# Threshold attention and a squared-ReLU MLP on one core: values taken one step later, and their loads moved behind the last placing

## The chip, the cores and the metric

The kernel runs on one core of a Trainium2 chip. The metric is the device time of one execution in microseconds. The kernel before takes 1539.25 us (median of three runs, 1538.57 to 1540.27); its profiled execution has a span of 1535.8 us.

## The reference

Two stages, all in 32-bit floats. The first is attention with a threshold: 8 batches of 8 heads, 576 rows of 64 elements each. A score counts only if it is within tau (0.02) of the largest of its row.

```python
scores = scale * np.matmul(q, k.transpose(0, 1, 3, 2))
thresh = np.max(scores, axis=-1, keepdims=True) - tau
scores = np.where(scores >= thresh, scores, -1000000000.0)
scores = scores - np.max(scores, axis=-1, keepdims=True)
attn = np.exp(scores)
attn = attn / (np.sum(attn, axis=-1, keepdims=True) + 1e-09)
attn_out = np.matmul(attn, v)
```

The second takes the heads of a token side by side as a row x of 512 elements (4608 tokens) and computes `np.maximum(x @ w_in, 0) ** 2 @ w_out`, with w_in 512 x 2048 and w_out 2048 x 512.

## The kernel before

**Visits and steps.** Two heads make a pair, and there are 32 pairs, four to a batch. A *visit* works on one pair; the first eight visits share out the first batch's four pairs, so there are 36 visits (n from 0). A whole visit has five *steps* (i from 0 to 4). Steps 0 to 3 take 128 queries of each head of the pair; step 4 takes the 64 queries that are left of both heads together, by way of the tile `qmid`, and so has half the work. Further down, "step 4" is always a visit's last.

**One step.** `scores` (L201) multiplies queries with all 576 keys into PSUM tiles s0 and s1, which exist once, and DVE takes each row's maximum (L206). `exponents` (ACT, L214 to L217) writes the exponentials to a tile w. `threshold` (DVE, L229 to L232) compares, masks and sums; after it s0 and s1 are free again. `divide` (GpSimd, L239 to L241) normalizes w.

**Turning the weights.** The product with the values needs w transposed, with keys on the partitions, in the tile `wT`, which exists once. In early visits PE does this. From visit 11 on (`by_dma(n)`: 25 visits) DVE turns blocks of 32 x 32 one step later (`turn_blocks`, L296) into the tile `turned`, and DMAs put them where they belong (`place_blocks`): when step 3 has been turned, which is in step 4, sixteen transfers place all the blocks of steps 0 to 3 at once (L307, 144 KB each), and when step 4 has been turned, which is in step 0 of the next visit, sixteen smaller ones place what is left (L314, 16 or 20 KB each). The blocks of step 4 are turned into the tile `ql`, which the queries came in and which is free by then.

**Taking the values.** `mix` (L357) multiplies `wT` with the values of the pair, `vs[n % 2]`, in 20 matmuls over two PSUM banks, and `put` copies the result to the ring `xT` (ACT, L333 to L344), from which the MLP reads. The lists `mixes` says in which step it is done: `mixed = {NBLK: (0, 4)}` means all columns at once, four steps after the visit's step 4, so in step 3 of the next visit. In the step's text it stands right behind `scores` and `exponents`.

**Loads.** All of these transfers are issued by the queue of the SP engine, one after another in the order of the program. Queries and keys of the next visit (`load_qk`, L162 and L164, ten transfers) are asked for in step 2 and transposed by DVE in step 4 (`prep`, L180), after `threshold` and ahead of that step's `turn_blocks`. Values (`load_v`, L172 and L175, six transfers) are asked for at the end of step 4, for the next visit; in the queue they stand behind L307 and ahead of L314.

**The MLP as a filling.** The tokens are cut into 18 chunks of 256. When the mix of a batch's last pair is done, its chunks are complete (`complete`, `chunk_at`) and their *pieces* are added to a waiting list: `mlp_in` (L399) and `product` (L466, seven products in place of eight on halves of the matrices), each of eight matmuls in the profile's count. `fill` emits pieces between the parts of a step, a quarter of the step's share each time. The share comes from `rate`: the work at hand, spread over the steps up to the next chunk, less `VALUES_US` (4.8) in a step that has a mix. `END` is the step of the last mix; what still waits then is emitted behind it.

The order of each engine's instructions is the order of this text (a manual schedule). A step's text, cut to the change:

```python
scores(s) ... exponents(n, i)
if s in mixes and not old:
    mix(*mixes[s])              # then add_chunk(...)
fill(quarter)
threshold(n, i); prep(n + 1)    # prep in step 4
turn_blocks(m, x)               # of the step before
if x >= NBLK - 1:
    place_blocks(m, x)
fill(quarter) ... divide(n, i) ... fill(quarter); fill(quarter)
elif last and more and n >= 2 * HP:
    load_v(n + 1)
```

Of the kernel before, what the change touches and what calls it, by code (L numbers as in the profile page):

```python
# [19 lines left out]
def kernel(  # L20
# [15 lines left out]
    HP = H // 2  # L36
    NPAIR = B * HP
    NBLK = S // P
# [39 lines left out]
    at = RAW * 2 * WP  # L78
# [45 lines left out]
    def round_weights(i, stage):  # L124

        words = weight_area(i).bitcast(U32).rearrange("p (n w) -> p n w", w=2)
        lo, hi = words[:, :, 0], words[:, :, 1]  # L130
        t, e, d = (turned[:, (i % 3 * 3 + x) * WP:(i % 3 * 3 + x + 1) * WP] for x in range(3))
        tu, eu = t.bitcast(U32), e.bitcast(U32)
        if stage == 0:
            nc.scalar.activation(out=e, in_=hi.bitcast(FP32), func=AF.Copy, scale=2.0 ** -112)
            nc.scalar.activation(out=d, in_=lo, func=AF.Copy, scale=2.0 ** -52)
        elif stage == 1:
            nc.vector.tensor_scalar(out=tu, in0=hi, scalar1=0x80000000, scalar2=None, op0=ALU.bitwise_and)
            nc.vector.scalar_tensor_tensor(out=tu, in0=eu, scalar=3, in1=tu, op0=ALU.logical_shift_left,  # L138
                                           op1=ALU.bitwise_or)
        elif stage == 2:  # L140
            nc.vector.tensor_scalar(out=eu, in0=tu, scalar1=0xFF800000, scalar2=None, op0=ALU.bitwise_and)  # L141
        elif stage == 3:
            nc.gpsimd.tensor_tensor(out=d, in0=d, in1=e, op=ALU.mult)  # L143
        else:
            nc.gpsimd.tensor_tensor(out=weight_piece(i)[1], in0=t.rearrange("p (h d) -> p h d", h=2),
                                    in1=d.rearrange("p (h d) -> p h d", h=2), op=ALU.add)
# [4 lines left out]
    def load_qk(n):  # L151


        b, h = divmod(visits[n][0], HP)
        h *= 2
        for x, t in list(zip(rows_of(n), (q, k)))[::-1]:
            for m in range(4):
                queue = nc.scalar if n == 0 and m % 2 else nc.sync
                src = t[b, h + m // 2, :, (m % 2) * 32:(m % 2) * 32 + 32].rearrange("(c p) d -> p c d", p=32)
                last = REST // 32 if t is k and m >= 2 else 0  # L160
                to = x[m * 32:(m + 1) * 32, :, :]
                queue.dma_start(out=to[:, last:, :], in_=src[:, 0:S // 32 - last, :])  # L162
                if last:
                    queue.dma_start(out=to[:, 0:last, :], in_=src[:, S // 32 - last:, :])  # L164
# [12 lines left out]
    def prep(n):  # L177

        for to, rows in zip((qT, kT), rows_of(n)):
            nc.vector.transpose(to, rows.rearrange("p c d -> p (c d)"))  # L180
        if NBLK in visits[n][1]:
            for u in range(2):
                rows = slice(u * D, (u + 1) * D)
                nc.gpsimd.tensor_copy(out=qmid[rows, u * D:(u + 1) * D], in_=qT[rows, NBLK * P:S])  # L184
# [3 lines left out]
    def scores(s):  # L188

        vis, i = steps[s]  # L190
        n = 2 if i < NBLK else 1
        sc = [psum.tile([P, 2, 512], FP32, tag=f"s{u}", name=f"s{u}") for u in range(n)]
        halves = [(half, u) for half in range(2) for u in range(n)]
        if early():
            halves.sort(key=lambda x: x[1])
        for half, u in halves:
            if i < NBLK:
                rows, lhsT = slice(u * D, (u + 1) * D), qT[u * D:(u + 1) * D, i * P:(i + 1) * P]
            else:
                rows, lhsT = slice(0, P), qmid  # L200
            nc.tensor.matmul(sc[u][:, half, 0:HALF], lhsT, kT[rows, half * HALF:(half + 1) * HALF],  # L201
                             start=True, stop=True)
        st = pool.tile([P, 7, 2], FP32, tag="st", name="st", bufs=4)
        mx = st[:, 0, 0:n]
        for u in range(n):
            nc.vector.tensor_reduce(out=mx[:, u:u + 1], in_=sc[u][:, :, 0:HALF], axis=AX.XY, op=ALU.max)  # L206

        w = w_slots[(s - first_dma) % (2 if by_dma(vis) else 3)][:, 0:n, :]
        weights[vis, i] = w, sc, st

    def exponents(vis, i):
        w, sc, st = weights[vis, i]
        mx, thr, bias = (st[:, j, 0:len(sc)] for j in range(3))
        nc.scalar.activation(out=bias, in_=mx, func=AF.Copy, scale=-SCALE)  # L214
        nc.scalar.activation(out=thr, in_=mx, func=AF.Identity, bias=ntau8)
        for u in range(len(sc)):
            nc.scalar.activation(out=w[:, u, :].rearrange("p (h k) -> p h k", h=2), in_=sc[u][:, :, 0:HALF],  # L217
                                 func=AF.Exp, bias=bias[:, u:u + 1], scale=SCALE)
# [288 lines left out]
    def by_dma(n):  # L507

        return n >= 3 * HP - 1
# [6 lines left out]
    for s, (n, i) in enumerate(steps):  # L516

        if by_dma(n):
            mixed = {NBLK: (0, 4)}
        else:  # L520
            mixed = {x: (x, 3) for x in range(NBLK + 1)}
        if i in mixed:
            first, lag = mixed[i]
            cols = slice(first * P, min((i + 1) * P, S))
            mixes[s + lag] = (n, cols)
            g_ = visits[n][0]
            if g_ % HP == HP - 1:
                complete[s + lag] = g_ // HP * S + cols.stop
# [12 lines left out]
    def early():  # L541
        return state["step"] < min(chunk_at)
# [10 lines left out]
    def add_chunk(j):  # L553
        waiting.extend(pieces_of(j))
# [65 lines left out]
    for s in range(END + 1):  # L620
        state["step"] = s
        state["usable"] = rounded_by[-1]
        rounded_by.append(state["rounded"])
        on = s < NST
        now = []
        if on:
            n, i = steps[s]
            at = visits[n][1].index(i)
            last = at == len(visits[n][1]) - 1
            now = list(range(done, done + pieces[s]))  # L630
            done += pieces[s]
            more = n + 1 < len(visits)
            short = n < 2 * HP
            if short and at == 0 and 0 < n + 1 < 2 * HP:
                load_qk(n + 2)
            elif not short and at == (2 if by_dma(n) else 1) and more:
                load_qk(n + 1)
            if now:
                round_weights(now[0], 0)
            scores(s)  # L640
        old = steps[s - 2] if 2 <= s < NST + 2 and not by_dma(steps[s - 2][0]) else None
        at_once = now or old or early()
        lay = on and last and more and not by_dma(n)
        if old:
            turn(*old, 0)
            turn(*old, 1)
        if on:
            exponents(n, i)
            if lay:
                prep(n + 1)  # L650
            elif now:
                round_weights(now[0], 1)
        if s in mixes and not old:
            mix(*mixes[s])
            for j in chunk_at.get(s, ()):
                add_chunk(j)
        quarter = rate(s) / 4 if s < END else 1e9
        fill(quarter)
        if s in mixes and old:
            mix(*mixes[s])  # L660
            for j in chunk_at.get(s, ()):
                add_chunk(j)
        if old:
            turn(*old, 2)
        state["free"] = s > first_dma
        if on:
            threshold(n, i)
            if last and more and not lay:
                prep(n + 1)
            if lay and now:  # L670
                round_weights(now[0], 1)
            if now:
                round_weights(now[0], 2)
                round_weights(now[0], 3)
            if not at_once:
                divide(n, i)
        if 0 < s <= NST and by_dma(steps[s - 1][0]):
            m, x = steps[s - 1]
            turn_blocks(m, x)
# [3 lines that stand above are left out]
        if on and at_once:  # L683
            divide(n, i)
        fill(quarter)
        fill(quarter)
        if on:
            if now:
                end_rounding(now[0])
            for p in now[1:]:  # L690
                for stage in range(4):
                    round_weights(p, stage)
                end_rounding(p)
            if at == 0 and 0 < n <= 2 * HP:
                load_v(n)
            elif last and more and n >= 2 * HP:
                load_v(n + 1)
    after()
    after()
# [33 lines left out]
```

## Time and profile before

| engine | busy us | share of the span |
|---|---|---|
| PE, matmuls | 1416.3 | 92% |
| PEld, weight loads | 1086.5 | 71% |
| DVE | 864.7 | 56% |
| GpSimd | 670.5 | 44% |
| ACT | 439.7 | 29% |

Weight loads run beside matmuls. Other rows of the page: L201 has 178.3 us of matmuls, L399 520.1 us, and L466 250.4 and 187.9 us in two groups. In the chain of work that ended last PE holds 42% of the span and the SP queue 31%: L307 17%, L314 14%.

Three stretches can be told apart. Up to about 280 us weights are loaded and rounded beside the first visits, and PE turns the blocks. From 278.42 us, the first placing by L307, to 1374 us the 25 visits by DMA run, each of some 44 us, with pieces of the MLP between their steps. From 1375 us only the MLP is left. A row of the timeline gives start and duration in us, the engine, the line and the operation, what is written from what, how many records are merged in it, and in brackets the idle time of the engine before it with what ended it. Rows of the SP queue are the times of issue; a transfer's landing comes later (median 3.5 us after the issue for wT<-turned, 1.8 to 1.9 us for wT<-ql, 2.4 us for ql<-in_q_dram).

### The profile page before, as it was taken

What the parts mean: (1) busy time and instruction counts of PE and PEld (TensorE: products, weight loads), DVE (VectorE), ACT (ScalarE), POOL (GpSimd) and SP (SyncE); (2) the same over time, 40 slices, a digit from 0 to 9 for tenths busy, and PEclk for the clock granted to TensorE, in tenths of its full rate; (3) what the DMA queues carried; (4) which work ended last, traced back from release to release, by engine and by line L of the source; (5) the groups of instructions that cost most, each with busy time, mean ns of one, the idle gap of its engine ahead of it and who ended that gap; (6) DMA issues with size and microseconds to landing.
All of it is one profiled execution on the core that took longest, in us unless ns stands there. A gap on an engine that the chain in (4) does not pass through costs nothing.

```text
span 1535.8 us, 21858 instructions
## 1 busy us (share of the span) xinstructions
PE 1416.3 (92%) x7460; PEld 1086.5 (71%) x7460; DVE 864.7 (56%) x1847; ACT 439.7 (29%) x1080; POOL 670.5 (44%) x865
## 2 busy tenths in 40 slices
PE   5899999898989899899998998999999989999998
PEld 3676557676767677677776776777777767688887
DVE  5998887864646565556565655656565546411011
ACT  3766553222222222222222222222222222201100
POOL 3688775534342434334443434343534342423322
PEclk9999999999999999999999999999999999999999
DMA  7653431454334544444445454434554433340000
GB/s 147 136 141 101 118 88 30 79 103 86 81 64 92 101 81 102 90 88 73 88 84 107 79 102 85 84 65 97 94 105 80 102 67 75 68 84 0 15 15 14
DMA packets 414399, 127.09 MB, mean 83 GB/s; under 512 B 292689, under 2 KB 407889, under 8 KB 414289
## 3 DMA queue, kind: packets, MB, share of 16 engines
q1 hardware_dynamic: 409008, 115.96, 38.8%
q0 software_dynamic: 2896, 9.44, 1.7%
q8 instruction: 60, 0.98, 0.3%
q10 hardware_dynamic: 2384, 0.30, 0.1%
q14 instruction: 51, 0.41, 0.1%
HBM read 49.81 MB, written 9.44 MB: 39 GB/s over the span
## 4 chain that ended last, share of the span: by engine, by line
PE 42%; SPq 31%; DVE 12%; DMA 7%; issue 5%; ACT 3%; POOL 1%; DVEq 0%; ACTq 0%; POOLq 0%
SPq L307 17%; SPq L314 14%; PE bank L357 11%; PE bank L399 11%; PE bank L466 11%; PE s L201 6%; DVE turned L296 3%; DMA vs<-in_v_dram 3%; DMA wT<-ql 3%; DVE w L229 2%; DVE st L206 2%; PE bank L433 1%; PE bank L265 1%; ACT w L217 1%; DVE turned L138 1%
## 5 line engine op out<-in xcount | busy, mean ns | idle before, releaser
L399 PE MATMUL bank<-xT,w_in_sb 128*128 128x256 f32 x2304 | 520.1, 382 | 1.8 <-ACT osb L440 1.8
L399 PEld LDWEIGHTS bank<-xT,w_in_sb 128*128 128x128 f32 x2304 | 432.3, 190 | 81.9 <-issue 22.1
L206 DVE TENSOR_REDUCE st<-s 128x1 f32<-128x576 f32 x288 | 206.5, 751 | 314.2 <-PE s L201 313.2
L357 PE MATMUL bank<-wT,vs 128*64 128x128 f32 (+7 forms) x1700 | 213.2, 395 | 73.8 <-DMA wT<-ql 70.8
L229 DVE SCALAR_TENSOR_TENSOR w<-s,st,w 128x576 f32<-128x576 f32 x269 | 210.2, 815 | 121.6 <-ACT w L217 121.3
L466 PE MATMUL bank<-wo,gsum 128*128 128x256 f32 x1088 | 250.4, 383 | 3.6 <-POOL gsum L389 3.5
L357 PEld LDWEIGHTS bank<-wT,vs 128*64 128x64 f32 (+1 forms) x1700 | 125.5, 150 | 163.8 <-issue 127.7
L241 POOL TENSOR_SCALAR w<-w,st 128x576 f32<-128x576 f32 x269 | 227.2, 852 | 28.9 <-DVE st L232 22.7
L410 POOL TENSOR_TENSOR g<-g 128x512 f32<-128x512 f32 x144 | 150.9, 1054 | 201.2 <-ACT g L409 201.0
L466 PEld LDWEIGHTS bank<-wo,gsum 128*128 128x128 f32 x1088 | 205.6, 191 | 42.3 <-issue 7.6
L201 PE MATMUL s<-kT,qT 64*128 64x288 f32 x1024 | 178.3, 439 | 34.1 <-DVE w L229 17.5
L214 ACT ACTIVATE st<-st 128x2 f32<-128x2 f32 (+1 forms) x160 | 32.7, 204 | 608.1 <-DVE st L206 607.5
L466 PE MATMUL bank<-wo,g 128*128 128x256 f32 x816 | 187.9, 381 | 0.0
L217 ACT ACTIVATE w<-s,st 128x576 f32<-128x576 f32 x269 | 184.3, 731 | 0.6 <-issue 0.3
L239 POOL TENSOR_SCALAR st<-st 128x2 f32<-128x2 f32 (+1 forms) x160 | 37.4, 234 | 321.5 <-DVE w L229 311.1
L466 PEld LDWEIGHTS bank<-wo,g 128*128 128x128 f32 x816 | 153.5, 190 | 28.1 <-issue 6.9
L296 DVE STREAM_TRANSPOSE turned<-w 128x576 f32<-128x576 f32 (+2 forms) x300 | 147.7, 543 | 43.7 <-DMA vs<-in_v_dram 42.8
L201 PEld LDWEIGHTS s<-kT,qT 64*128 64x128 f32 x1024 | 100.3, 190 | 96.2 <-issue 67.1
L409 ACT ACTIVATE g<-bank 128x512 f32<-128x512 f32 x144 | 85.9, 599 | 176.9 <-PE bank L399 176.5
L480 DVE TENSOR_TENSOR gsum<-g 128x512 f32<-128x512 f32 x34 | 23.4, 718 | 111.5 <-PE bank L466 111.5
L184 POOL COPY qmid<-qT 64x64 f32<-64x64 f32 x64 | 18.7, 292 | 121.3 <-DVE qT L180 119.5
L143 POOL TENSOR_TENSOR turned<-turned 128x512 f32<-128x512 f32 x32 | 41.1, 1284 | 45.6 <-DVE turned L141 44.0
(67 smaller groups left out, 917.4 us busy)
## 6 DMA issues: line engine op xcount, KB each, us to landing
wT<-turned SPq DMA_DIRECT2D x400, 144.0 KB, 3.5
vs<-in_v_dram SPq DMA_DIRECT2D x72, 128.0 KB, 3.1
ql<-in_q_dram SPq DMA_DIRECT2D x126, 72.0 KB, 2.4
out_dram<-osb POOLq DMA_DIRECT2D x34, 256.0 KB, 2.8
wo<-in_moe_w_in_dram SPq DMA_DIRECT2D x16, 512.0 KB, 4.6
wo<-in_moe_w_out_dram SPq DMA_DIRECT2D x16, 512.0 KB, 3.8
kl<-in_k_dram SPq DMA_DIRECT2D x63, 72.0 KB, 2.3
kl<-in_k_dram SPq DMA_DIRECT2D x63, 64.0 KB, 2.3
```

Of the source, the lines that this page charges most:

```text
L201: nc.tensor.matmul(sc[u][:, half, 0:HALF], lhsT, kT[rows, half * HALF:(half + 1) * HALF], start=True, stop=True)
L206: nc.vector.tensor_reduce(out=mx[:, u:u + 1], in_=sc[u][:, :, 0:HALF], axis=AX.XY, op=ALU.max)
L217: nc.scalar.activation(out=w[:, u, :].rearrange("p (h k) -> p h k", h=2), in_=sc[u][:, :, 0:HALF], func=AF.Exp, bias=bias[:, u:u + 1], sca ...
L229: nc.vector.scalar_tensor_tensor(out=wu, in0=sc[u][:, :, 0:HALF], scalar=thr[:, u:u + 1], in1=wu, op0=ALU.is_ge, op1=ALU.mult, accum_out=s ...
L241: nc.gpsimd.tensor_scalar(out=w[:, u, :], in0=w[:, u, :], scalar1=z[:, u:u + 1], scalar2=rcp[:, u:u + 1], op0=ALU.add, op1=ALU.mult)
L296: nc.vector.transpose(to, w[:, u, k0 * 32:k1 * 32].rearrange("p (k q) -> p k q", q=32))
L307: nc.sync.dma_start(out=to[:, :, qb * P:(qb + 1) * P], in_=wb[rows, j::4, :])
L314: nc.sync.dma_start(out=to[:, c:c + n, at:at + 32], in_=wb[rows, first::4, :])
L357: nc.tensor.matmul(to, vs[n % 2][rows, u * (NBLK + 1) + c, :], mov, start=first, stop=last)
L399: nc.tensor.matmul(h[:, x % 2, :], w_in_sb[:, c, f * P:(f + 1) * P], xT[:, c, at:at + TCH], start=(c == 0), stop=(c == NMC - 1))
L410: nc.gpsimd.tensor_tensor(out=to, in0=to, in1=to, op=ALU.mult)
L466: nc.tensor.matmul(to, left[:, f, :], wo[:, slot, f, :], start=(f == 0), stop=(f == HF - 1))
```

## The change

The mix is done five steps after the visit's last step instead of four, which is in step 4 of the next visit, behind the scores and in the same step in which the next visit's blocks are placed into `wT`. In the visits by DMA the loads of values move from the end of step 4 to the end of step 0, behind the placing of what is left (L314). The change is meant to give the placing more time before its result is needed, and to let L314 start without six loads ahead of it.

```diff
         if by_dma(n):
-            mixed = {NBLK: (0, 4)}
+            mixed = {NBLK: (0, NBLK + 1)}
         else:
             mixed = {x: (x, 3) for x in range(NBLK + 1)}
...
-            if at == 0 and 0 < n <= 2 * HP:
+            if at == 0 and (0 < n <= 2 * HP or by_dma(n)):
                 load_v(n)
-            elif last and more and n >= 2 * HP:
+            elif last and more and n >= 2 * HP and not by_dma(n + 1):
                 load_v(n + 1)
```

## The prediction

> **What bounds the kernel now.** I read the page first: which engine is fullest, and what its idle time waits for.
>
> ```profile
> PE 1416.3 (92%) x7460; PEld 1086.5 (71%) x7460; DVE 864.7 (56%) x1847; ACT 439.7 (29%) x1080; POOL 670.5 (44%) x865
> L399 PE MATMUL bank<-xT,w_in_sb 128*128 128x256 f32 x2304 | 520.1, 382 | 1.8 <-ACT osb L440 1.8
> L357 PE MATMUL bank<-wT,vs 128*64 128x128 f32 (+7 forms) x1700 | 213.2, 395 | 73.8 <-DMA wT<-ql 70.8
> ```
>
> PE is the full engine, and of its matmul groups only L357, the taking of values (call it the mix), waits long: 70.8 us for the transfer wT<-ql, which is the placing of a visit's last block. All idle time of PE from 300 to 1400 us is 72.3 us (1100 less the sum of the busy column of eleven windows of 100 us), so in that stretch hardly anything else stops PE.
>
> Then four visits by themselves. A visit runs from one start of the 16 placing transfers of L307 to the next; columns are the busy time of the engines, the granted clock, the DMA share and GB/s.
>
> ```profile
> 721.58:764.39 42.81, 41.23 (x213) 31.99 (x213) 27.32 (x61) 10.62 (x26) 14.17 (x23) 1.00 0.49 97
> 764.39:807.60 43.21, 42.12 (x218) 32.49 (x217) 26.61 (x58) 11.22 (x28) 20.75 (x27) 1.00 0.45 84
> 854.57:898.98 44.41, 41.23 (x216) 31.56 (x215) 26.81 (x60) 10.14 (x28) 17.03 (x24) 1.00 0.44 81
> 807.60:854.57 46.97, 42.07 (x209) 32.38 (x210) 24.62 (x56) 11.80 (x28) 17.64 (x26) 0.96 0.44 88
> ```
>
> PE works 41 to 42 us in each, and the rest of the visit is the wait. DVE is at 27 us at most, the DMA engines below half. The last row also has a lower clock. The timeline of that visit, first the SP queue, then PE, then DVE in its last step:
>
> ```profile
> 807.60 13.20 SPq L307 DMA_DIRECT2D wT<-turned  x16
> 820.84 0.79 SPq L172 DMA_DIRECT2D vs<-in_v_dram  x1
> ...
> 825.71 10.34 SPq L314 DMA_DIRECT2D wT<-ql  x16
> 836.10 1.67 SPq L162 DMA_DIRECT2D kl<-in_k_dram  x3
> ...
> 839.34 2.05 SPq L162 DMA_DIRECT2D ql<-in_q_dram  x4
> 854.57 12.66 SPq L307 DMA_DIRECT2D wT<-turned  x16
> ```
>
> ```profile
> 832.28 0.72 PE L357 MATMUL bank<-wT,vs 128*64 128x320 f32 x2 [0.44 <-DMA wT<-ql]
> 837.46 6.44 PE L357 MATMUL bank<-wT,vs 128*64 128x320 f32 x38 [4.45 <-DMA wT<-ql]
> 843.83 3.72 PE L399 MATMUL bank<-xT,w_in_sb 128*128 128x256 f32 x16
> 847.38 1.13 PE L201 MATMUL s<-kT,qmid 128*128 128x288 f32 x4
> ```
>
> ```profile
> 848.55 0.76 DVE L206 TENSOR_REDUCE st<-s 128x1 f32<-128x576 f32 x1 [10.75 <-PE s L201]
> ...
> 851.63 0.78 DVE L180 STREAM_TRANSPOSE qT<-ql 128x576 f32<-128x576 f32 x1
> 852.33 0.73 DVE L180 STREAM_TRANSPOSE kT<-kl 128x576 f32<-128x576 f32 x1
> 852.99 1.51 DVE L296 STREAM_TRANSPOSE turned<-w 128x512 f32<-128x512 f32 x4
> ```
>
> The reader should see a ring. L307 issues for 13.2 us, six loads of values stand behind it for 4.9 us (820.84 to 825.71), L314 issues for 10.3 us and lands near 837.3. Only then can PE do the mix, some pieces, and the last step's scores (847.38); these let DVE turn the blocks that the next L307 at 854.57 places. The SP queue is idle from 841.4 to 854.6, so it isn't full either: each of the two waits for the other once per visit.
>
> **What the Trainium skill says.** "TensorE: Matmul & The Clock Gate", the section on HAM oscillation, asks for no PE gaps longer than about 3.4 us, since the clock is then halved until PE has been busy again. The trace agrees: the mix's 38 records take 4.75 us after all waits under 1.6 us (and once after 3.18), but 6.1 us or more after every other wait of 2 to 4.5 us; so the trace's limit is nearer 2 us. "Perfetto Trace Analysis", DMA Instruction — HWDGE, says that the issuing sequencer does its semaphore wait before it issues and goes to its next instruction only after that; so a waiting placing holds back all loads behind it. The SP rows above do stand strictly one behind another. "DMA: Bandwidth & Descriptors", Two DMAs through the same engine are not ordered, says that only the completion semaphore orders a transfer; here the placing's landing after its last issue costs 1.9 us, the page's median.
>
> **The change, part by part.**
> 1. *The mix moves from step 3 of the next visit to step 4, behind its scores.* Same matmuls, so no work is added. L314 lands at 837.3, and with the scores of step 4 out at 848.3 (847.38 plus 0.97) PE would come to the mix about 11 us later than the landing, which moves 4.9 us earlier besides (part 4); when the visit has shrunk by some 6 us, 10 us are left. The 70.8 us (25 visits, 2.8 us each) vanish.
> 2. *The half clock behind these waits goes with them.* Rows of 38 records with a long wait against 4.75 us: sixteen of the 24 visits from 346 us on show an excess, 1.3 to 2.6 us each, in sum 27.3 us (2.34+1.33+1.36+1.41+1.54+2.64+1.48+ nine of 1.69). I take 27; nought would be the other end, if the clock fell for another reason, and would give 1473.
> 3. *The next L307 now waits for the mix.* It overwrites wT, which the mix reads. What is queued behind it on SP is everything: L314, the values, the next q and k. The mix starts 0.97 us behind the start of the scores and takes 5.47 us (0.72 plus 4.75), so it ends 6.4 us after that start. L307 already starts 7.2 us after it (854.57 less 847.38), waiting for DVE's turning. The wait is hidden by 0.8 us: nothing. If it were not, at most 1 us a visit on SP.
> 4. *The loads of values go behind L314.* Same transfers, so SP works as long; L314 starts 4.9 us earlier, and q and k at the same place as before. The values are used only in the last step of the visit after. Nothing.
> 5. *The planner.* It leaves room for the mix in the step where the mix stands, so pieces move from step 4 to step 3; in the emitted order of the changed kernel steps 0 to 3 carry 3 or 4 pieces (5.45 or 7.17 us for 24 or 32 records) and step 4 none to two. Chunks of the MLP come one step later and one filling step is added at the end; both are the same work on a PE that has pieces waiting. Nothing.
> 6. *A ring that was slack comes near.* From an L307 to the next one goes another way: SP issues L307, values, L314, k and q (33.5 us, mean of ten visits, from 367.67 to 797.64 us), q lands (2.4 us, page median), DVE transposes q and k (1.5), turns the block (1.5), and the next L307 goes: 39 us with hand-overs. PE's visit: four times 1.17 for scores plus 0.97, a mix of 5.5, and pieces of 1.79 us. The emitted order has 15 pieces in seven of the first nine visits and 16 in two (38.0 and 39.8 us), later mostly 17 (41.6 us). In those seven the loads would be 1.0 us late, 7 us in all; less 2.3 us that DVE has in hand: its next maximum is due 9.5 us after step 4's scores start (0.97, mix 5.47, a pair of pieces 1.8, scores 1.24), and it has turned the block by 7.2. That leaves 5 us.
>
> Sum: 1539.25 - 70.8 - 27.3 + 5 = 1446. I choose that one.
>
> **The rivals.**
> - *Loads stretch, the ring of part 6 binds.* Against it, the DMA share is 0.44 to 0.49 in these visits; for it, the issues of L307 already vary from 12.5 to 14.2 us, and the same bytes go in a tenth less time. At 41 us a visit the first nine lose 2.6 us each, 23 us: 1464. At 42 us, with 0.5 us for the others: 1481.
> - *Half of the waits come back.* PE has no more pauses in which ACT, POOL and DVE catch up; squares (L410) or freed banks would then be awaited. Against it: in 721 to 807 us PE waits little more than 1 us a visit and nothing else appears. Half of 98 us back: 1490.
> - *Slower.* The mix ends late, L307 waits for it, with all loads behind it, and q and k come after DVE wants them, so that the ring is over the present mean of 44.45 us ((1345.29 - 278.42)/24). It needs some 6 us on the 39 of part 6. At 45 us: 1539 + 24 x 0.55 = 1552. The 0.8 us of part 3 are thin, but being late there costs one such lateness, not six.
>
> **How the numbers follow.** 0.62 for the forecast with its bounds (no lateness of the loads gives 1441, twice of it 1451), 0.19 for the stretched loads, 0.11 for half of the waits, 0.04 for slower, and 0.04 for better than 1434, if the waits also hide lost time among the pieces behind the mix. The range takes the forecast and most of the first rival: 1434 to 1472. Faster by over 0.2%: 0.95; within it 0.01; slower 0.04.
>
> **What would show it.** Part 1: the group L357 has less than 5 us of idle before it by wT<-ql, and the landing of L314 lies well before the mix. Part 2: clock 0.99 or 1.00 from 350 to 1340 us and all rows of 38 records near 4.75 us. Part 3: SP's wait of L307 is still put down to DVE's L296, or to PE's L357 by tenths of a microsecond. Part 6: DVE's L180 waits for ql or kl in the visits before about 700 us and not after; their period is near 39 us, later near 41.6. It is wrong if L180, or scores behind it, wait in most visits, if L307 waits over 1 us for PE, or if PE has new idle time on ACT or POOL that adds to over 20 us.

## The result, and the profile after

The changed kernel takes 1441.24 us (median, 1438.57 to 1441.78) against 1539.76 us on the same chip: a ratio of 0.9356, with a 95% interval of 0.934 to 0.9372. The forecast was 1446 us. The profiled execution has a span of 1440.0 us, 95.8 less than before.

From the page of the changed kernel, engine totals and the group of the mix:

```profile
PE 1382.3 (96%) x7460; PEld 1058.8 (74%) x7460; DVE 864.2 (60%) x1847; ACT 440.2 (31%) x1080; POOL 671.8 (47%) x865
L357 PE MATMUL bank<-wT,vs 128*64 128x128 f32 (+7 forms) x1700 | 169.4, 358 | 2.6 <-ACT wT L266 2.4
```

The matmul records are the same 7460. The mix no longer waits for any transfer: the 70.8 us for wT<-ql are gone, and what is left is 2.6 us from the early visits. Its busy time fell as well, by 43.8 us (213.2 - 169.4). So of the 95.8 us, 61.8 are idle time of PE (119.5 before, 57.7 now) and 34.0 are busy time in which PE did no more work than it does now.

The timeline of a visit, the SP queue first and then PE:

```profile
837.76 13.67 SPq L307 DMA_DIRECT2D wT<-turned  x16
851.53 10.28 SPq L314 DMA_DIRECT2D wT<-ql  x16
861.85 0.59 SPq L172 DMA_DIRECT2D vs<-in_v_dram  x1
...
868.76 2.04 SPq L162 DMA_DIRECT2D ql<-in_q_dram  x4
878.47 6.92 SPq L307 DMA_DIRECT2D wT<-turned  x9
```

```profile
830.57 1.13 PE L201 MATMUL s<-kT,qmid 128*128 128x288 f32 x4
831.63 4.79 PE L357 MATMUL bank<-wT,vs 128*64 128x320 f32 x40
836.35 1.99 PE L466 MATMUL bank<-wo,gsum 128*128 128x256 f32 x8
...
871.28 1.13 PE L201 MATMUL s<-kT,qmid 128*128 128x288 f32 x4
872.34 4.79 PE L357 MATMUL bank<-wT,vs 128*64 128x320 f32 x40
```

Here L314 follows L307 at once, its last issue ends at 861.8, and PE comes to the mix at 872.34, some 9 us after the landing. All 40 records of a mix are now one row of 4.79 us, with nothing in brackets. The mix that starts at 831.63 is over at 836.42, and the L307 which overwrites what it read starts at 837.76, so that wait is hidden by 1.3 us.

Three visits of the changed kernel (length, busy PE, PEld, DVE, ACT and POOL, clock, DMA share, GB/s):

```profile
437.59:476.90 39.31, 38.47 (x201) 28.89 (x198) 26.85 (x61) 9.61 (x26) 15.62 (x23) 1.00 0.51 99
594.08:635.86 41.78, 38.29 (x187) 28.33 (x187) 27.38 (x61) 9.55 (x25) 14.90 (x22) 0.96 0.48 93
635.86:676.57 40.71, 40.71 (x214) 31.36 (x213) 23.20 (x53) 12.76 (x30) 22.66 (x29) 1.00 0.49 95
```

The last is the usual visit from 636 us on: PE has work in every microsecond of it. The first two are from the first nine visits and of another kind; PE is idle for 0.8 and 3.5 us in them, and the second has a half clock too. Who is waited for in 300 to 1300 us (total us, times, longest), two lines of DVE's waits and two of PE's:

```profile
DVE turned L296 <- DMA wT<-ql: 43.5, 22, 5.0
DVE qT L180 <- DMA ql<-in_q_dram: 10.5, 5, 3.2
PE s L201 <- DVE w L229: 4.7, 3, 2.3
PE s L201 <- DVE kT L180: 1.6, 2, 1.2
```

DVE stands twice: for q (L180), and for the tile `turned`, which L307 must have read before step 0's block can be turned into it (L296; the name wT<-ql is only that of the transfer which follows on the queue: in seven of the first eight of these waits L296 starts 0.18 us after the last landing of L307). PE gets a little of either.

### The profile page after: what moved, and what is told of

The parts are those of the page before. It is cut to its first block, busy times and chain, and to the rows that moved or that the text cites. A ratio compares the mean times of both kernels' runs of the same rounds, so it can differ in the third digit from the quotient of the medians.

```text
span 1440.0 us, 21857 instructions
## 1 busy us (share of the span) xinstructions
PE 1382.3 (96%) x7460; PEld 1058.8 (74%) x7460; DVE 864.2 (60%) x1847; ACT 440.2 (31%) x1080; POOL 671.8 (47%) x865
## 4 chain that ended last, share of the span: by engine, by line
PE 71%; SPq 12%; DVE 8%; issue 3%; ACT 2%; DMA 2%; POOL 1%; DVEq 0%; ACTq 0%; POOLq 0%
PE bank L399 28%; PE bank L466 22%; PE s L201 10%; PE bank L357 8%; SPq L307 5%; SPq L314 4%; SPq L162 2%; DVE st L206 1%; PE bank L265 1%; DVE w L229 1%; DVE turned L138 1%; PE bank L433 1%; SPq L175 1%; DVE turned L296 1%; DMA ql<-in_q_dram 1%
## 5 line engine op out<-in xcount | busy, mean ns | idle before, releaser
L229 DVE SCALAR_TENSOR_TENSOR w<-s,st,w 128x576 f32<-128x576 f32 x269 | 210.1, 815 | 121.2 <-ACT w L217 120.9
L466 PE MATMUL bank<-wo,gsum 128*128 128x256 f32 x1088 | 252.5, 385 | 6.4 <-POOL gsum L389 5.1
L466 PEld LDWEIGHTS bank<-wo,gsum 128*128 128x128 f32 x1088 | 204.6, 191 | 49.0 <-issue 11.4
L201 PE MATMUL s<-kT,qT 64*128 64x288 f32 x1024 | 182.2, 444 | 40.5 <-DVE w L229 19.4
L466 PE MATMUL bank<-wo,g 128*128 128x256 f32 x816 | 189.2, 384 | 0.0
L466 PEld LDWEIGHTS bank<-wo,g 128*128 128x128 f32 x816 | 154.4, 191 | 29.7 <-issue 7.8
L296 DVE STREAM_TRANSPOSE turned<-w 128x576 f32<-128x576 f32 (+2 forms) x300 | 147.7, 543 | 45.3 <-DMA wT<-ql 45.1
L357 PE MATMUL bank<-wT,vs 128*64 128x128 f32 (+7 forms) x1700 | 169.4, 358 | 2.6 <-ACT wT L266 2.4
L357 PEld LDWEIGHTS bank<-wT,vs 128*64 128x64 f32 (+1 forms) x1700 | 96.8, 138 | 76.4 <-issue 25.8
L184 POOL COPY qmid<-qT 64x64 f32<-64x64 f32 x64 | 18.8, 293 | 90.4 <-DVE qT L180 88.5
```

The lines of the kernel that those rows point to most:

```text
L229: nc.vector.scalar_tensor_tensor(out=wu, in0=sc[u][:, :, 0:HALF], scalar=thr[:, u:u + 1], in1=wu, op0=ALU.is_ge, op1=ALU.mult, accum_out=s ...
L296: nc.vector.transpose(to, w[:, u, k0 * 32:k1 * 32].rearrange("p (k q) -> p k q", q=32))
L357: nc.tensor.matmul(to, vs[n % 2][rows, u * (NBLK + 1) + c, :], mov, start=first, stop=last)
L466: nc.tensor.matmul(to, left[:, f, :], wo[:, slot, f, :], start=(f == 0), stop=(f == HF - 1))
```

## The experiments

Times are medians with lowest and highest; a ratio under 1 is faster. The first four kernels of the table ran on the same chip, and so did the next four, and the last three; the kernel before was at 1541 to 1543 us beside them.

| kernel | us | ratio to before, 95% interval |
|---|---|---|
| mix later alone | 1441.98 (1440.51 to 1445.66) | 0.9369 (0.9335 to 0.9403) |
| loads moved alone | 1439.92 (1436.48 to 1441.68) | 0.9356 (0.9317 to 0.9395) |
| before, PE kept busy in the wait | 1523.70 (1521.30 to 1529.26) | 0.9900 (0.9865 to 0.9935) |
| changed, pieces ahead of the mix | 1445.06 (1441.91 to 1445.17) | 0.9380 (0.9348 to 0.9413) |
| changed, q and k first | 1429.27 (1426.90 to 1431.52) | 0.9271 (0.9240 to 0.9302) |
| changed, block 0 turned later | 1434.71 (1430.94 to 1437.32) | 0.9309 (0.9278 to 0.9339) |
| changed, both of these | 1425.20 (1423.17 to 1430.09) | 0.9248 (0.9219 to 0.9278) |
| changed, again | 1442.09 (1439.03 to 1442.64) | 0.9348 (0.9317 to 0.9379) |
| loads moved, q and k first, mix in step 3 | 1435.05 (1430.96 to 1443.22) | 0.9316 (0.9273 to 0.9358) |
| changed, q and k first, again | 1427.08 (1423.39 to 1431.24) | 0.9250 (0.9214 to 0.9286) |
| changed, both, again | 1428.24 (1422.85 to 1429.32) | 0.9251 (0.9216 to 0.9286) |

**Each half of the change by itself.** The mix later alone:

```diff
-            mixed = {NBLK: (0, 4)}
+            mixed = {NBLK: (0, NBLK + 1)}
```

> The mix one step later, the loads of values where they were, ahead of L314. Theory (two rings: L307 - L314 - landing - mix - scores - L307, opened by the later mix; and L307 - all loads - q and k landed - L307 at 39 us, under PE's visit): L314 lands 4.9 us later than in the changed kernel, but still some 5 us ahead of the mix, so nothing is lost: 1441 us, within 5 us of the changed kernel, and no idle time of L357 put down to wT<-ql. Rival (the two edits share the gain, because the mix needs L314 early as well): L357 waits 1 to 2 us in most visits, 1465 to 1490 us.

The loads moved alone are the other two lines of the change:

```diff
-            if at == 0 and 0 < n <= 2 * HP:
+            if at == 0 and (0 < n <= 2 * HP or by_dma(n)):
...
-            elif last and more and n >= 2 * HP:
+            elif last and more and n >= 2 * HP and not by_dma(n + 1):
```

> The loads of values behind L314, the mix where it was, in step 3. Theory (the ring through the mix is shortened by the 4.9 us of issues): L307 13.0, L314 10.7, landing 1.2, mix 4.8, one piece 1.8, step 4 up to the next L307 7.2, together 38.7 us, under PE's 40.7 us a visit; so L357 waits under 1 us a visit, mostly in the first nine, and the time is 1441 to 1455 us: this edit alone would do nearly as much as both. Rival (only the later mix takes the wait away): more than half of the 70.8 us stays, 1490 us or more.

Either half gives what both give; the three can't be told apart by these times. What is waited for is not the same, though. With the mix later alone L357 has no wait for the placing. With the loads alone some of it stays, in mixes like this one, from PE's timeline:

```profile
340.62 0.75 PE L357 MATMUL bank<-wT,vs 128*64 128x320 f32 x2
344.34 6.44 PE L357 MATMUL bank<-wT,vs 128*64 128x320 f32 x38 [2.97 <-DMA wT<-ql]
```

and in sum, from PE's waits in 300 to 1400 us:

```profile
PE bank L357 <- DMA wT<-ql: 9.9, 7, 3.0
```

What follows: the 44.45 us of a visit before were the ring through the mix, and both edits loosen that same ring, one by about 5 us and the other by a whole step. Behind it comes PE's own work, 40.7 us in most visits from the tenth on; in the first nine, where PE has only 37 to 39 us to do, a ring through the queue still binds a little (below). Either edit is enough to get there, so the gains are the same gain; they don't add. The rivals, by which the halves share it, fell.

**The half clock.** The kernel before, with matmuls that depend on nothing new in front of each mix:

```diff
         N1 = 2 * P + REST
+        for d in range(6):
+            nc.tensor.matmul(one[:, 0:2 * P], w_in_sb[:, 0, 0:P], w_in_sb[:, 1, 0:2 * P], start=True, stop=True)
```

> The kernel before, with six matmuls of 128x256 added ahead of each mix by DMA, into the bank that the mix overwrites, which wait for nothing that the mix waits for (12 records, 2.7 us a visit, 25 visits, 67 us of added work; output unchanged). Theory (the half clock behind the waits is a cost of its own, set off by idle PE): the half clocks from 350 to 1340 us go from 65 us to under 20 us, rows of 38 records come down to 4.8 us, and the kernel is faster than the one before in spite of the added work, about 1521 us. Rival (the slow rows come from late operands, not from the clock): rows stay at 6.4 us in half of the visits and the time is 1540 to 1560 us.

With 300 matmul records more the kernel is 1.0% faster (interval 0.65 to 1.35%), at 1523.7 us where 1521 was expected. The half clocks recorded from 350 to 1340 us are 6.8 us in all, in place of 64.4. Two mixes of PE's timeline:

```profile
439.68 4.75 PE L357 MATMUL bank<-wT,vs 128*64 128x320 f32 x38 [2.72 <-DMA wT<-ql]
...
526.17 6.44 PE L357 MATMUL bank<-wT,vs 128*64 128x320 f32 x38 [2.70 <-DMA wT<-ql]
```

So the slow rows were the clock's doing and idle PE was its cause. The second row has 3.41 us of half clock in it, and half of that is what it takes beyond 4.75 us. The two rows also show that the length of a wait doesn't decide alone: nearly equal waits, one with and one without.

What differs is where they lie. In the trace of every kernel of this case the half clocks begin on a grid of 3.413 us. Windows of that grid at the two waits, with their length, the busy time of PE (records in brackets) and the clock; DMA share and GB/s behind it don't matter here:

```profile
434.98:438.39 3.41, 1.98 (x8) 1.00 0.19 31
438.39:441.80 3.41, 2.12 (x18) 1.00 0.48 78
...
523.73:527.14 3.41, 0.97 (x8) 1.00 0.34 56
527.14:530.55 3.41, 3.41 (x16) 0.50 0.49 78
```

The first wait is cut by the grid, so that PE is idle for 1.43 us of one window and 1.29 us of the next. The second leaves 2.44 us of one window idle, and the window behind it has the half clock. From 300 to 1380 us of the thirteen traces, each of the 25 windows with 2.01 us or more of idle PE is followed by one of half clock; of the 4076 with 1.97 us or less five are, three of them at half clock already. That is a pattern in the traces: no run moved a wait against the grid to test it.

**How thin the new wait is.** In the changed kernel, the filling pieces of step 4 go ahead of the mix:

```diff
...
+        if late:
+            fill(4 * quarter)
+            quarter = 0.0
+            mix(*mixes[s])
...
```

> The changed kernel, with the filling pieces of step 4 emitted ahead of the mix instead of behind it (mostly one piece, 1.8 us, in some visits two or none), so that the mix ends about 1.0 us, with two pieces 2.8 us, after DVE has turned the blocks, and L307 waits for PE that long. Theory (what stands behind L307 has slack against PE's 40.7 us only as far as the 39 us of its own ring): L307's wait is put down to PE's L357, the ring is 40 us; nothing is lost in the later visits and 1 to 2 us in each of the first nine: 1448 to 1460 us. Rival (a wait put on the SP queue costs its whole length each visit): 25 visits of 1 to 2.8 us, 1470 us or more. Second rival: L307 has slack everywhere: 1441 us.

The SP queue's waits in 300 to 1300 us:

```profile
SPq L307 <- DVE turned L296: 159.7, 24, 12.4
SPq L307 <- PE bank L357: 11.4, 14, 2.2
```

In the changed kernel the second line is 0.2 us, so the wait was made, 0.8 us in the mean of 14. It cost at most a few microseconds: 1445 us against 1442 for the mix later alone on the same chip, with ranges that overlap. That a wait on the queue costs its full length each visit (1470 us or more) is refuted; between the theory, whose 1448 us are not reached either, and no cost at all, this run doesn't decide.

**What binds in the first visits of the changed kernel.** Two candidates: late q and k, or DVE at L296. The first is taken away by asking for q and k in step 1, ahead of the values:

```diff
-            elif not short and at == (2 if by_dma(n) else 1) and more:
+            elif not short and at == 1 and more:
                 load_qk(n + 1)
...
-            if at == 0 and (0 < n <= 2 * HP or by_dma(n)):
+            if at == 0 and 0 < n <= 2 * HP or at == 1 and by_dma(n):
                 load_v(n)
```

> The changed kernel, with q and k asked for in step 1 instead of 2 and the values behind them, at the end of step 1, so that the queue runs L307 - L314 - k, q - values and q lands 4.1 us earlier. Theory (what is left of PE's idle time in 300 to 1300 us comes from DVE's L296, which waits for L307 to have read turned, and not from late loads): L180's wait for ql (10.5 us in that stretch) goes to about 0, but only 1.6 us of PE's idle time goes with it: 1440 us, the same as the changed kernel within its noise. Rival (the prediction's part 6: late loads cost the 5 us): 1435 us or less.

The second by turning step 0's block a step later:

```diff
             scores(s)
+            if s >= 2 and by_dma(steps[s - 2][0]) and steps[s - 2][1] == 0:
+                turn_blocks(*steps[s - 2])
...
-            turn_blocks(m, x)
+            if x:
+                turn_blocks(m, x)
```

> The changed kernel, with the turning of step 0's block (two of L296's instructions, 1.4 us) put one step later, behind the maxima of step 2 and ahead of step 1's turning, so that DVE no longer stands at L296 for L307's landing with the sums of step 2 queued behind. Theory: L296's wait for the DMA (43.5 us in 300 to 1300 us) goes to under 10 us, PE's waits for L229 (4.7 us, and the half clock behind them, 5 us) go; the exponents of step 2 start up to 1.4 us later, which PE doesn't see: 1432 us. Rival (these waits are DVE's own overload in visits with L480 and L484, whatever L296 waits for): same as the changed kernel or slower, since step 2 gets 1.4 us longer on DVE: 1441 us or more.

Both edits together:

> Both of these edits: the two gains add if they are apart: 1431 us, PE idle in 300 to 1300 us under 5 us. If both only shift the same wait it is no better than the better of the two.

The changed kernel beside these three:

> The changed kernel once more, on the same chip as the three others, to compare with: 1441 us, within 3 us of its first time.

My theory fell. Asking for q and k first, which I had expected to do nothing, took 12.8 us off (1442.09 to 1429.27, ranges apart). Its waits of DVE and PE in 300 to 1300 us:

```profile
DVE turned L296 <- DMA wT<-ql: 32.3, 22, 3.6
...
PE s L201 <- DVE w L229: 1.4, 1, 1.4
```

and one of its early visits, in the columns of the visits above:

```profile
394.60:431.84 37.24, 37.24 (x198) 28.31 (x197) 23.18 (x53) 12.19 (x30) 18.32 (x26) 1.00 0.55 111
```

L180 no longer waits for any load, and the wait of L296 fell with it, to 32.3 us from 43.5 (42.6 in the changed kernel's trace on the same chip), although nothing was done about it: late q holds DVE at L180, DVE then turns the block late, L307 starts late, and its landing holds DVE again at L296 a step and a half later. The wait that PE showed (L229) stood at the end of that chain, and I had put it down to the last link. By the starts of L307 the first nine visits take 344.4 us (623.38 - 278.99), and 357.8 us (636.21 - 278.38) in the changed kernel on the same chip; the fifteen behind them take 609.0 us in both, so the whole gain lies in the first nine. Between these two traces PE's idle time in 300 to 1300 us went from 10.2 to 4.5 us, and 10.2 us of half clock went to none.

Turning the block later cut the chain at its last link. L296's wait for the transfer is gone, and the kernel is 7 us faster than the changed one (1434.71 against 1442.09, ranges apart), but DVE stands at the first link for longer:

```profile
DVE qT L180 <- DMA ql<-in_q_dram: 17.0, 9, 4.0
...
PE s L201 <- DVE kT L180: 3.0, 3, 2.0
```

Both edits together are not better than q and k first by anything that these runs can tell; the first time 1425.20 against 1429.27, and in a second set, of which these were the expectations, the other way round (1428.24 against 1427.08):

> The changed kernel with q and k ahead of the values once more, to compare on one chip: 1429 us. First eight visits 38.1 us each, as in its first run.

> The same with the turning of step 0's block one step later, once more: if that edit is worth something beside the earlier q and k it is the 2.2 us of the one visit in which L229 still holds PE up, 1427 us; if not, 1429 us.

**What the later mix is worth once the loads don't bind.** The loads moved and q and k first, but the mix in step 3 as before:

> The loads of values behind L314, q and k ahead of them in step 1, but the mix where it was before the change, in step 3. It tells what the later mix is worth once the loads no longer bind. Theory (two rings of nearly the same length; opening one leaves the other): the ring through the mix, 38.7 us by the working for the kernel with the loads alone moved, still binds in the first eight visits, where PE's own work is 38 to 39.8 us; L357 waits for wT<-ql in several of them, about 10 us in sum as there, and the time is 1434 to 1440 us, 5 us or more above the same edit with the later mix (1429 us). Rival (the ring through the mix has slack enough): 1429 us, the later mix adds nothing.

PE's waits in 300 to 1300 us:

```profile
PE bank L357 <- DMA wT<-ql: 8.8, 7, 1.9
```

The wait for the placing is there as expected, and the first eight visits take 39.57 us ((589.14 - 272.59)/8) against 38.07 with the later mix on the same chip ((578.00 - 273.43)/8). The medians are 8 us apart, in the direction expected (1435.05 and 1427.08), but the ranges touch, so the traces show the mechanism better than the times show its size. The best kernels are the changed one with q and k first, at 1429.27 and 1427.08 us (ratios of 0.9271 and 0.9250), and the one with both edits, which can't be told apart from it.

## Why the prediction was right, and where it was off

- **Part 1, the wait for the placing: right.** 70.8 us to nothing (24 of the 25 mixes had waited); L314 lands 9 us ahead of the mix, where 10 were worked out.
- **Part 2, the half clock: right.** From 300 to 1400 us the half clocks recorded fall from 64.8 to 10.2 us, and the kernel with PE kept busy in the wait shows the cause by itself.
- **Part 3, L307 behind the mix: right** for this place (1.3 us in hand in the visit shown, 0.8 worked out; SP's wait for L357 is 0.2 us in all).
- **Part 4, loads of values: "nothing" is right beside part 1**, as the kernel with the mix later alone shows. It leaves out that this edit alone would have done the same.
- **Part 5: right in the main.** Most visits from the tenth on take 40.7 us with all their pieces. "Nothing" is not quite it: PE's waits at the products (L466) in 300 to 1300 us went from 1.2 to 4.0 us.
- **Part 6, the loads: the mechanism was right, its 5 us were too small.** L180 waits for ql in visits before 600 us and in none behind them, as forecast, and taking the late loads away gives 12.8 us. Two of its terms failed.

  The first is the mix, which was put at 5.47 us (0.72 + 4.75) where it takes 4.72 (836.35 less 831.63). In the kernel before, from the start of a mix to the start of what follows, each of the 24 mixes with a wait took 0.65 to 0.71 us more than 4.72 us, its idle time and half of its half clock together: part of the loss stands in the rows as busy time. So a visit of 15 pieces takes PE 37.24 us, not 38.0, and one of 17 takes 40.71, not 41.6; with loads near 39.3 us (mean of the first eight visits in the changed kernel's second trace) the lateness in a visit of 15 is some 2 us, not 1.

  The second is the 2.3 us that DVE was said to have in hand. They count one consumer of late loads, its own next maximum; the way through L307 and L296 into step 2 was left out. ("A pair of pieces 1.8" in that sum is the time of one piece.)
- **That the sum came out so near is in part luck.** The same mis-sized term is a gain that the sum left out: of the 43.8 us by which L357's busy time fell only 27.3 are the slow rows, and the other 16.5 us, 0.69 for each of the 24 waits, are what the rows hid. Against that, more was lost again than 5 us. Between the two profiles PE's idle time apart from the wait for the placing grew by 9.0 us (70.8 - 61.8), and the busy time of its other groups by 9.8 us (43.8 - 34.0); half clocks of 10.2 us can be up to 5 of these, and the rest is not explained. So there were 18.8 us of loss where 5 were put down, against 16.5 us of gain not seen: two errors that nearly cancel.
- **Rivals.** Stretched loads (1464) didn't come about as such: L307's issues still take 12.6 to 14.3 us. But the ring that this rival named did bind in the first nine visits, at 39.8 us each in place of its 41, and the 12.8 us which that cost lie between the forecast's 5 and the rival's 23. Half of the waits coming back (1490) and slower (1552) were wide of it.

## What to carry to other kernels

When an engine waits once in each round, write down the whole ring that it is in, through queue, landing and the other engines, and then the next ring and the engine's own work; a cut anywhere in the longest ring gives the same gain, and only down to the second longest. Edits that loosen the same ring don't add, so try each alone. A small wait that shows at the end of a chain can be the last link of a longer one: ask what the thing waited for was itself waiting for, and look at the period of the round instead of the sum of idle times.

## What the runs showed of the hardware that was not expected

- Half clocks set in behind waits of little over 2 us: after 2.02 and 2.04 us in the kernel before, and not after 3.18 us in another of its visits. What told them apart in these traces was the idle time within one window of a 3.413 us grid: 2.01 us or more was followed by half clock each time, and the wait of 3.18 us was cut into 1.64 and 1.54 us.
- PE rows next to a wait are longer than their work: 0.72 us for two records and 4.75 us for the other 38, where all 40 together take 4.79. In this kernel the trace's idle time of PE was short of the true loss by about 0.69 us a wait.
